# Packing six of eight head groups' outputs densely for the last query block's output projection

## The chip, the cores and the metric

The kernel runs on one core of one Trainium2 chip. The metric is the device time of one execution in microseconds; lower is better. Where several runs are given, the median is meant. TensorE is called PE, VectorE DVE, ScalarE ACT, GpSimd POOL and SyncE SP, as the profile does.

## What is computed

One transformer layer over 2048 tokens of width 640: layer norm, attention with 32 heads of 20 columns each, an output projection with `wo`, a residual sum; then a second layer norm, a bilinear GLU with hidden width 1728, its down projection and a second residual sum. Everything is bfloat16 from outside. The reference, cut:

```python
def _A_ref(x, wqkv, wo):
    qkv = (x @ wqkv).reshape(B, S, 3, H, Dh).transpose(2, 0, 3, 1, 4)
    q, k, v = qkv[0], qkv[1], qkv[2]
    p = softmax(einsum("bhqd,bhkd->bhqk", q, k) * (Dh ** -0.5))
    o = einsum("bhqk,bhkd->bhqd", p, v)
    return o.transpose(0, 2, 1, 3).reshape(B, S, D) @ wo
def _B_ref(x, w_gate, w_up, w_down):
    return ((x @ w_gate) * (x @ w_up)) @ w_down
h = x + _A_ref(layernorm(x), wqkv, wo)
out = h + _B_ref(layernorm(h), w_gate, w_up, w_down)
```

## The kernel before, in words

**Tiling.** The 2048 queries are four blocks of 512. The 32 heads are eight groups of four. A head has 20 rows, but it sits in a slot of 32 of the 128 partitions (`SLOT`), so that four heads fill one tile and PE can take a head's 32 rows alone; 12 rows of each slot are padding. Scores are computed transposed (128 keys by queries): L557 writes three banks of 512 columns of a score tile, ACT turns them into exponentials (L573), and L795 multiplies them with the values into the accumulator `acc`. Where the planner finds DVE free, one of the three banks is exponentiated by DVE instead with four operations (L610, L620, L621, L615), and ACT's instruction has 1024 columns instead of 1536.

**Passes.** The last block is block 3. Its group 0 is computed for all 512 queries (pass "3"), and groups 1 to 7 first for the first half of 256 queries (pass "A"), then for the second half (pass "B").

**Normalising.** The row sums of the softmax come out of the same matmul as the values. For most groups `norm` (L659) sends them out to DRAM (`sums`, L666) and back in another shape (`sums_all`, L667), takes reciprocals on DVE (L677), sends these out (`scr`, L679) and back to 32 partitions each (`bc`, four DMAs, L682), and then multiplies (L685) into `On[g]`, a 128 x 512 tile for each group, still in slots of 32 rows. The product is put in line seven score tiles later; the queue of DVE side work decides when it is done. Groups 7 of pass "A" and 6 and 7 of pass "B" are normalised without DRAM, by matmuls with an identity (L700, L716, L731, and L1391 in the tail).

**Projection.** `wo[g]` holds the output weights with the same padding: zeros, and 20 rows for each head (L987, L991). `out_mm` (L1047) adds eight matmuls for a tile of 128 queries and half of the 640 columns (L1052), and DVE adds the residual. For the first half of block 3 this is done by `job_quick`, which then takes the layer norm at once, while attention of pass "B" goes on. The second half is left to the tail.

**Tail.** `last_tail` (L1366) runs when all exponentials are done. For each of two tiles of queries and two halves of columns, `out_most` adds the residual by an identity matmul (L1376) and seven groups (L1378); `out_last` adds group 7 (L1382), which is normalised meanwhile: PE collects the sums (L700), DVE takes reciprocals and spreads them (L708, L710), PE turns them (L716), DVE multiplies (L1391). Then follow statistics (L209), the layer norm, the transposes, the GLU (L1203) and the down projection (L1270). Behind the projection stand 14 matmuls of a down projection held back for this, and warming matmuls (L1414), beside the layer norm.

**What sets the order.** The order on all engines is written by a planner in the kernel while the program is built: it keeps a model of the time at which PE, DVE and ACT get free, and puts jobs (projections, GLU, down projections) on PE between score tiles where its model leaves room. `later(n, fn)` lets something happen n score tiles later. Where PE's dense work gets thin in the model, it adds matmuls that keep PE's clock up (L508 and L553). All DMAs but the instruction loads go through SP's one queue, in program order; SP waits for what a DMA needs, and everything behind it waits too.

**Weights of the tail.** `load_last` (L1356) loads the rows of x for the last two tiles of queries and the GLU weights of parts 0 and 1 (four DMAs of 320 KB). The tail's GLU reads the resident parts 3 to 6 first, then 0, 1 and 2.

Of the kernel before, what the change touches and what calls it, by code (L numbers as in the profile page):

```python
# [10 lines left out]
BF16 = mybir.dt.bfloat16  # L11
# [5 lines left out]
ALU = mybir.AluOpType  # L17
AX = mybir.AxisListType

P = 128  # L20
# [3 lines left out]
DH = 20  # L24
NT = S // P
KT = D // P
FF = 1728
SLOT = 32
HPG = 4
NG = H // HPG  # L30
# [8 lines left out]
HALF = D // 2  # L39
FP = 7  # L40
FPW = 256
G1 = 4
SPLIT_G = {"1": 4, "2": 2, "3": 1}
QA = 3 * QB
RES0 = 3
# [29 lines left out]
ALONE_NS = {"out": 4350, "glu": 15260, "y": 5710}  # L75
PART_NS, TILE_NS, ROOM = 31500, 700, 2500
E_BUFS, E_LATE = 6, 2
SHIFT = 544.0
LOG2E = 1.4426950408889634
X_UNIT = 128.0  # L80
# [11 lines left out]
def kernel(  # L92
# [11 lines left out]
    nc = tc.nc  # L104
# [32 lines left out]
    wo = [const.tile([P, D], BF16, name=f"wo{g}") for g in range(NG)]  # L137
# [8 lines left out]
    On = [onp.tile([P, QB], BF16, name=f"on{g}") for g in range(NG)]  # L146
# [201 lines left out]
    for s, (p, g, lo, hi, _) in enumerate(segs):  # L348
        w = PASS[p][2]
        n = BANK // w  # L350
# [46 lines left out]
    def later(n, fn):  # L397
        events.append((now["i"] + n, fn))
# [257 lines left out]
    def read_out(b):  # L656
        return all(("om", b, t) in done for t in TAILS[b])

    def norm(s, asb):  # L659
        p, g = segs[s][0:2]  # L660
        b, c0, w = PASS[p]
        n = w // 32
        r16 = sums_all[:, col["n"]:col["n"] + n]
        col["n"] += n
        sums = dram.tile([HPG, w], F32, name="sums", tag=f"sums{w}")
        nc.sync.dma_start(sums[:], asb[DH:P:SLOT, 0:w])  # L666
        nc.sync.dma_start(r16, sums[:].rearrange("j (c f) -> (j c) f", f=n))  # L667

        due = at["dve"] + SUMS_NS

        def back():
            if at["pe"] < due and now["i"] < n_tiles:
                later(1, back)
                return
            ri = nrm.tile([P, n], F32, name="ri", tag=f"ri{n}")
            dve(130)
            nc.vector.reciprocal(ri[:], r16)  # L677
            scr = dram.tile([HPG, w], F32, name="scr", tag=f"scr{w}")
            nc.sync.dma_start(scr[:].rearrange("j (c f) -> (j c) f", f=n), ri[:])  # L679
            bc = nrm.tile([P, QB], F32, name="bc")  # L680
            for j in range(HPG):
                nc.sync.dma_start(bc[SLOT * j:SLOT * (j + 1), 0:w], scr[j:j + 1, :].to_broadcast([SLOT, w]))  # L682

            def times(asb, bc, p, g, c0, w):
                nc.vector.tensor_tensor(On[g][:, c0:c0 + w], asb[:, 0:w], bc[:, 0:w], ALU.mult)  # L685
                done.add(("n", p, g))
                yield 605 * w // QB

            def mult():
                if b and not read_out(b - 1):  # L690
                    later(1, mult)
                    return
                aux.append(times(asb, bc, p, g, c0, w))
            later(7, mult)
        later(4, back)
# [173 lines left out]
    m32, r = rstd_act(pair_mv[0], 2, lambda: bn(pair_mv[1], 0, xs[0][:, 2, :]))  # L869
# [11 lines left out]
    m32, r = rstd_act(pair_mv[1], 2)  # L881
# [103 lines left out]
    def load_wo():  # L985
        for g in range(NG):
# [6 lines left out]
            while at["pe"] < due and not now["forced"]:  # L993
                yield WAIT

    def make_identf():
        nc.vector.tensor_copy(identf[:], ident[:])

# [14 lines left out]
    late = {"res": {}, "next": {}}  # L1013
# [15 lines left out]
            nc.gpsimd.memset(late["Wd"][f][0:p0, :], 0.0)  # L1029
        nc.sync.dma_start(late["Wd"][f][p0:P, :], B_w_down[f * P:f * P + P - p0, :])  # L1030

    def new_st(rows_of):
        st = {"rows": rows_of, "xr": {}, "ln2T": late["ln2T"]}
        return st

    def load_tail(st, ts):
# [10 lines left out]
    def out_mm(on, st, t):  # L1047
        for hf in range(2):
            ps = bank()
            cs = slice(hf * HALF, (hf + 1) * HALF)  # L1050
            for g in range(NG):
                nc.tensor.matmul(ps[:, 0:HALF], lhsT=on[g][:, t * P:(t + 1) * P], rhs=wo[g][:, cs],  # L1052
                                 start=(g == 0), stop=(g == NG - 1))
                if g == NG - 1:
                    dve(408, 136)
                    nc.vector.tensor_tensor(st["h"][t][:, cs], ps[:, 0:HALF], st["xr"][t][:, cs], ALU.add)  # L1056
                yield 136
            done.add(("oh", t, hf))
            yield NEXT
# [76 lines left out]
    def job_out(on, st, ts, key):  # L1136
        pairs = [ts[k:k + 2] for k in range(0, len(ts), 2)]

        def T_pair(pair):
            for t in pair:  # L1140
                while end["pool"] is None and key is not None and (
                        ("l2", key, t) not in done or key in COLUMNS_OF and ("glu",) + COLUMNS_OF[key] not in done):
                    yield WAIT
                ensure_aux(("l2", key, t))
                if key is None:
                    yield from job_T(st["l", t], st["ln2T"][:, :, t * P:(t + 1) * P])
                    yield NEXT
                else:
                    nc.sync.dma_start(st["ln2T"][:, :, t * P:(t + 1) * P], st["l", t][:], transpose=True)
                    l2_at[key, t] = max(at["pe"], l2_at[key, t]) + TURN_NS  # L1150
            for t in pair:
                while end["pool"] is None and key is not None and at["pe"] < l2_at[key, t]:
                    yield WAIT
                ln2["rows"] -= 1
        done.difference_update({("l2", key, t) for t in ts})
        for k, pair in enumerate(pairs):
            for t in pair:
                yield from out_mm(on, st, t)
            if key is not None and k == len(pairs) - 1:
                done.add(("om",) + key)  # L1160
            aux.append(ln2_pieces(st, pair, key))
            if k:
                yield from T_pair(pairs[k - 1])
        yield from T_pair(pairs[-1])

    def w_tile(src, fp, wt):
        w = min(FPW, FF - fp * FPW)
        view = wt[:, 0:KT * FPW].rearrange("p (c f) -> p c f", f=FPW)
        nc.sync.dma_start(view[:, :, 0:w], src[:, fp * FPW:fp * FPW + w].rearrange("(c p) f -> p c f", p=P))
# [124 lines left out]

    def rows(b, ts):
        if b not in tail_st:
            tail_st[b] = new_st(rows_of(b))
            tail_st[b]["res"] = late["res"]
        load_tail(tail_st[b], ts)
        rows_in.add((b, ts[0]))  # L1300
# [55 lines left out]
    def load_last():  # L1356
        st = tail_st[LAST_B]
        load_tail(st, LAST_T)
        load_w(0, st)
        load_w(1, st)  # L1360

    def run(gen):
        for _ in gen:
# [2 lines left out]
    def last_tail():  # L1366
# [6 lines left out]
        def out_most(t, hf):  # L1373
            ps = ps_h[t, hf] = bank()
            cs = slice(hf * HALF, (hf + 1) * HALF)
            nc.tensor.matmul(ps[:, 0:HALF], lhsT=ident[:], rhs=st["xr"][t][:, cs], start=True, stop=False)  # L1376
            for g in range(NG - 1):
                nc.tensor.matmul(ps[:, 0:HALF], lhsT=on[g][:, t * P:(t + 1) * P], rhs=wo[g][:, cs], start=False, stop=False)  # L1378

        def out_last(t):  # L1380
            for hf in range(2):
# [131 lines left out]


    def general():
        st = new_st(None)
        st["res"] = {}
        with tc.For_i(0, S, P) as r0:
            st["rows"] = lambda t: bass.ds(r0, P)
# [2 lines left out]
            for g in range(NG):  # L1522
# [42 lines left out]
                nc.vector.tensor_copy(On[g][:, 0:P], ps[:])  # L1565
# [36 lines left out]
```

## Time and profile before

| | |
|---|---|
| median of 3 runs | 896.7 us (895.01 to 898.06) |
| the profiled execution | 900.67 us |
| its span, first to last instruction | 898.8 us |
| mean granted clock of PE | 0.989 |
| end of the last exponential | about 858.8 us |
| tail behind it | about 35 us |

The profile is one execution. Busy time is counted per engine; a line such as L573 is a line of the kernel; "idle before" is idle time of the engine just ahead of an instruction and what ended it. The granted clock is the share of full speed that PE was given. Matmul ends are modelled, so a group of pipelined matmuls is best read by the distance between starts. In a row with "x7" the length covers all seven. The planner's stretch of pass "A" and "B" and the tail are the parts that matter here.

### The profile page before, as it was taken

The page shows a single profiled execution, that of the slowest core. Times are in us where ns is not written, and L with a number is a line of the kernel's source. Part 1 is how long each engine was busy: PE and PEld are TensorE (multiplying, and loading weights), DVE is VectorE, ACT ScalarE, POOL GpSimd, SP SyncE. Part 2 cuts the span into 40 slices and gives each one's busy share as a digit, 9 for nine tenths or more (in the row PEclk, how much of TensorE's full clock was granted, in tenths as well). Part 3 has the DMA queues.
Part 4 walks back from the last instruction along what each step waited for, and adds up shares of the span by engine and source line. Part 5 has one row for each costly group of instructions (what it writes and reads, how often), then busy time and mean ns, then how long its engine had stood idle before and what let it go on. Part 6 is the DMA issues. An engine that isn't in the chain of part 4 may idle for free.

```text
span 898.8 us, 21965 instructions
## 1 busy us (share of the span) xinstructions
PE 813.7 (91%) x8921; PEld 374.1 (42%) x8921; DVE 773.7 (86%) x1448; ACT 852.7 (95%) x719; POOL 31.4 (3%) x122
## 2 busy tenths in 40 slices
PE   7889999989999899889999998998899999999997
PEld 5333232222233344544444554443434455444465
DVE  7778899999999899789999998999889988889842
ACT  6999999999999999989999999999999999999951
POOL 4100000000002000001000000001000000000000
PEclk9999999999999999989999999999989999999999
DMA  6030010011034556432214334111441312010310
GB/s 198 25 65 2 1 28 25 15 36 28 14 84 112 122 146 198 112 88 66 54 51 122 81 96 107 47 30 29 121 121 45 85 31 74 15 44 9 94 38 18
DMA packets 110763, 60.15 MB, mean 67 GB/s; under 512 B 37976, under 2 KB 107652, under 8 KB 110656
## 3 DMA queue, kind: packets, MB, share of 16 engines
q1 hardware_dynamic: 110656, 58.68, 25.0%
q8 instruction: 72, 1.18, 0.6%
q14 instruction: 35, 0.29, 0.1%
HBM read 48.09 MB, written 7.28 MB: 62 GB/s over the span
## 4 chain that ended last, share of the span: by engine, by line
ACT 56%; PE 21%; issue 13%; DVE 9%; DMA 1%; SPq 0%; ACTq 0%; DVEq 0%
ACT E L573 46%; ACT El L573 10%; PE sc L557 5%; PE mi L1221 3%; PE acc L795 3%; PE f L1203 2%; PE mi L306 1%; PE mi L1052 1%; DVE xv L610 1%; PE mi L1270 1%; PE f L1270 1%; DVE xt L620 1%; DVE xt L621 1%; DVE xe L615 1%; DVE hh L1229 1%
## 5 line engine op out<-in xcount | busy, mean ns | idle before, releaser
L573 ACT ACTIVATE E<-sc 128x1536 bf16<-128x1536 f32 (+1 forms) x560 | 694.0, 1387 | 7.3 <-PE sc L557 6.0
L557 PE MATMUL sc<-qa,kT 32*128 32x256 bf16 (+1 forms) x2176 | 204.1, 320 | 23.8 <-ACT E L573 13.5
L557 PEld LDWEIGHTS <-kT 32*128 32x128 bf16 x3136 | 85.2, 92 | 223.9 <-issue 193.4
L610 DVE TENSOR_SCALAR xv<-sc 128x512 f32<-128x512 f32 x199 | 137.1, 690 | 47.3 <-PE sc L557 44.4
L573 ACT ACTIVATE El<-sc 128x1536 bf16<-128x1536 f32 (+1 forms) x123 | 159.7, 1371 | 0.6 <-PE sc L557 0.5
L795 PE MATMUL acc<-E,vx 128*32 128x256 bf16 (+1 forms) x2245 | 158.2, 315 | 0.6 <-DVE vx L271 0.6
L615 DVE SCALAR_TENSOR_TENSOR xe<-xt,xv 128x512 int16<-128x512 f32 x199 | 134.3, 681 | 0.8
L621 DVE SCALAR_TENSOR_TENSOR xt<-xt,xv 128x512 f32<-128x512 f32 x199 | 133.2, 680 | 0.6
L620 DVE SCALAR_TENSOR_TENSOR xt<-xv 128x512 f32<-128x512 uint16 x199 | 132.1, 679 | 0.3 <-DVE ri L677 0.2
L306 PE MATMUL mi<-lnT,wp 128*128 128x512 bf16 x305 | 86.5, 381 | 7.1 <-DVE qa L313 3.4
L795 PEld LDWEIGHTS <-vx 128*32 128x32 bf16 x3136 | 62.2, 96 | 62.5 <-issue 60.6
L557 PE MATMUL sc<-qb,kT 32*128 32x256 bf16 (+1 forms) x960 | 69.0, 283 | 3.4 <-ACT E L573 2.2
L1270 PE MATMUL mi<-wd,hh 128*128 128x320 bf16 x378 | 65.5, 301 | 1.1 <-DVE xr L1274 1.0
L1221 PE MATMUL mi<-ln2T,wg 128*128 128x256 bf16 x390 | 56.7, 274 | 8.6 <-DVE u L1226 7.2
L1221 PE MATMUL mi<-ln2T,wu 128*128 128x256 bf16 x390 | 55.5, 274 | 7.4 <-DVE hh L1229 7.2
L795 PE MATMUL acc<-El,vx 128*32 128x256 bf16 (+1 forms) x579 | 60.6, 294 | 0.5 <-ACT El L573 0.5
L795 PE MATMUL acc<-xe,vx 128*32 128x256 bf16 (+1 forms) x312 | 57.3, 306 | 0.0
L1270 PEld LDWEIGHTS <-hh 128*128 128x128 bf16 x448 | 37.9, 97 | 29.5 <-issue 18.2
L1221 PEld LDWEIGHTS <-wg 128*128 128x128 bf16 x390 | 33.6, 97 | 30.0 <-issue 25.3
L306 PEld LDWEIGHTS <-wp 128*128 128x128 bf16 x310 | 24.8, 97 | 50.6 <-issue 38.5
L1221 PEld LDWEIGHTS <-wu 128*128 128x128 bf16 x390 | 33.8, 97 | 28.3 <-issue 25.1
L1052 PE MATMUL mi<-wo,on 128*128 128x320 bf16 x224 | 41.6, 312 | 2.3 <-DVE xr L1056 2.2
(152 smaller groups left out, 623.0 us busy)
## 6 DMA issues: line engine op xcount, KB each, us to landing
wu<-in_B_w_up_dram SPq DMA_DIRECT2D x38, 320.0 KB
wg<-in_B_w_gate_dram SPq DMA_DIRECT2D x37, 320.0 KB
bc<-scr SPq DMA_DIRECT2D x60, 64.0 KB
bc<-scr SPq DMA_DIRECT2D x108, 32.0 KB
qsp<-qa SPq DMA_DIRECT2D x8, 384.0 KB
xr<-in_A_x_dram SPq DMA_DIRECT2D x16, 160.0 KB
out_dram<-xr SPq DMA_DIRECT2D x14, 160.0 KB
wd<-in_B_w_down_dram SPq DMA_DIRECT2D x13, 160.0 KB
```

The costliest lines, as they stand in the source:

```text
L306: nc.tensor.matmul(ps[:], lhsT=wslice(m, g, c), rhs=lnT[:, c, ch * QB:(ch + 1) * QB], start=(c == 0), stop=(c == KT - 1))
L557: nc.tensor.matmul(sc[:, o:o + w], lhsT=kT[g][SLOT * j:SLOT * (j + 1), kt * P:(kt + 1) * P], rhs=q_of(g, b, c0, w)[SLOT * j:SLOT * (j + 1) ...
L573: exps = nc.scalar.activation(e[:, 0:n_act], sc[:, 0:n_act], ACT.Exp, bias=EXP_BIAS, scale=SM_SCALE)
L610: took = nc.vector.tensor_scalar(v[:], ps, X_SCALE, X_BASE, ALU.mult, ALU.max)
L615: nc.vector.scalar_tensor_tensor(e[:], t[:], X_R, v[:], ALU.mult, ALU.add)
L620: lambda: nc.vector.scalar_tensor_tensor(t[:], u, X_P, u, ALU.add, ALU.mult),
L621: lambda: nc.vector.scalar_tensor_tensor(t[:], t[:], X_Q, u, ALU.add, ALU.mult),
L795: nc.tensor.matmul(acc["t"][SLOT * j:SLOT * (j + 1), 0:w], lhsT=vx[kt][:, VS * h:VS * h + SLOT], rhs=e, start=(acc["n"][j] == 0), stop=(ac ...
L1052: nc.tensor.matmul(ps[:, 0:HALF], lhsT=on[g][:, t * P:(t + 1) * P], rhs=wo[g][:, cs], start=(g == 0), stop=(g == NG - 1))
L1203: nc.tensor.matmul(ps[:, 0:n], lhsT=st["w", fp][k][:, c, f_cols(fp, f2)], rhs=st["ln2T"][:, c, c0:c0 + n], start=(c == 0), stop=(c == KT - 1))
L1221: nc.tensor.matmul(ps[:, f2 * n:(f2 + 1) * n], lhsT=st["w", fp][k][:, c, f_cols(fp, f2)], rhs=st["ln2T"][:, c, c0:c0 + n], start=(c == 0), ...
L1270: nc.tensor.matmul(ps[:, 0:HALF], lhsT=st["hh"][f // 2][:, f % 2, t * P % HW:t * P % HW + P], rhs=late["Wd"][f][:, cs], start=(f == 0), st ...
```

## The change

Only the last block, and there only groups 0 to 5 (24 heads, 480 rows). The product L685 of such a group no longer goes to `On[g]` but to `On[4]` or `On[5]`, by turns. From there `pack` sends each head's 20 rows by DMA to their dense place: row 20 h of a stack of `On[0]` to `On[3]`. Where a head crosses a multiple of 128 it takes two DMAs. `On[0]` to `On[3]` then hold 128, 128, 128 and 96 rows without padding. The padded weights `wo[0]` to `wo[3]` are overwritten with 480 dense rows, three to six score tiles after the last projection of block 2. The projections of block 3 then add six terms (four dense ones, and groups 6 and 7 as before) instead of eight, the tail's `out_most` five instead of seven. Groups 6 and 7 are not packed. The fallback `general` is changed in the same way; it does not run on these inputs.

The four weight loads of `load_last` are no longer issued together, but 0, 3, 6 and 9 score tiles later.

```diff
+N_PACK = 6
+PACKED_ROWS = (128, 128, 128, 96)
+WO_AT, LAST_STEPS = 3, 3
...
+    def pack(o, g, cols):
+        for j in range(HPG):
+            r, d = DH * (HPG * g + j), 0
+            while d < DH:
+                to = (r + d) % P
+                n = min(DH - d, P - to)
+                nc.sync.dma_start(On[(r + d) // P][to:to + n, cols], o[SLOT * j + d:SLOT * j + d + n, cols])
+                d += n
...
             def times(asb, bc, p, g, c0, w):
-                nc.vector.tensor_tensor(On[g][:, c0:c0 + w], asb[:, 0:w], bc[:, 0:w], ALU.mult)
+                packed = b == LAST_B and g < N_PACK
+                o = On[4 + g % 2 if packed else g]
+                nc.vector.tensor_tensor(o[:, c0:c0 + w], asb[:, 0:w], bc[:, 0:w], ALU.mult)
+                if packed:
+                    pack(o, g, slice(c0, c0 + w))
...
+    def load_packed(k):
+        nc.sync.dma_start(wo[k][0:PACKED_ROWS[k], :], A_wo[P * k:P * k + PACKED_ROWS[k], :])
+
+    def out_terms(packed):
+        return [(k, n) for k, n in enumerate(PACKED_ROWS)] + [(g, P) for g in range(N_PACK, NG)] if packed else [(g, P) for g in range(NG)]
...
-            for g in range(NG):
-                nc.tensor.matmul(ps[:, 0:HALF], lhsT=on[g][:, t * P:(t + 1) * P], rhs=wo[g][:, cs],
+            for g, n in out_terms(st["packed"]):
+                nc.tensor.matmul(ps[:, 0:HALF], lhsT=on[g][0:n, t * P:(t + 1) * P], rhs=wo[g][0:n, cs],
...
                 done.add(("om",) + key)
+                if key == (LAST_B - 1, 2):
+                    for n in range(len(PACKED_ROWS)):
+                        later(WO_AT + n, lambda n=n: load_packed(n))
...
-        load_w(0, st)
-        load_w(1, st)
+        for fp in range(2):
+            two = st["w", fp] = []
+            for m, src in enumerate((B_w_up, B_w_gate)):
+                later(LAST_STEPS * (2 * fp + m), lambda fp=fp, src=src, nm=("wu", "wg")[m], two=two: two.append(
+                    w_tile(src, fp, late["w"].tile([P, KT * FPW], BF16, name=nm))))
...
-            for g in range(NG - 1):
-                nc.tensor.matmul(ps[:, 0:HALF], lhsT=on[g][:, t * P:(t + 1) * P], rhs=wo[g][:, cs], start=False, stop=False)
+            for g, n in out_terms(True)[:-1]:
+                nc.tensor.matmul(ps[:, 0:HALF], lhsT=on[g][0:n, t * P:(t + 1) * P], rhs=wo[g][0:n, cs], start=False, stop=False)
```

More of the change, by code (lines that the diff above doesn't have):

```diff
@@ L1030, in load_wd, with new_st @@
         nc.sync.dma_start(late["Wd"][f][p0:P, :], B_w_down[f * P:f * P + P - p0, :])
-    def new_st(rows_of):
-        st = {"rows": rows_of, "xr": {}, "ln2T": late["ln2T"]}
+    def new_st(rows_of, packed):
+        st = {"rows": rows_of, "xr": {}, "ln2T": late["ln2T"], "packed": packed}
         return st
@@ L1296, in rows @@
         if b not in tail_st:
-            tail_st[b] = new_st(rows_of(b))
+            tail_st[b] = new_st(rows_of(b), b == LAST_B)
             tail_st[b]["res"] = late["res"]
@@ L1515, in general @@
     def general():
-        st = new_st(None)
+        st = new_st(None, True)
         st["res"] = {}
@@ L1564, in general @@
                 nc.tensor.transpose(ps[:], oq[:].rearrange("p j e -> p (j e)"), ident[:])
-                nc.vector.tensor_copy(On[g][:, 0:P], ps[:])
+                o_t = On[4 + g % 2 if g < N_PACK else g]
+                nc.vector.tensor_copy(o_t[:, 0:P], ps[:])
+                if g < N_PACK:
+                    pack(o_t, g, slice(0, P))
             for fn in (job_out(On, st, [0], None), job_glu(st, [0]), job_y(st, [0])):
```

## The prediction

> **What bounds the kernel now.** I read the page first: its first line, the busy shares, and the group of the projection's matmuls.
>
> ```profile
> span 898.8 us, 21965 instructions
> PE 813.7 (91%) x8921; PEld 374.1 (42%) x8921; DVE 773.7 (86%) x1448; ACT 852.7 (95%) x719; POOL 31.4 (3%) x122
> L1052 PE MATMUL mi<-wo,on 128*128 128x320 bf16 x224 | 41.6, 312 | 2.3 <-DVE xr L1056 2.2
> ```
>
> ACT, which makes the exponentials, is busy 95%, PE 91%: an average that says nothing about the stage that is changed. The change takes 8 of the 224 projection matmuls of L1052 away, and 8 of the tail's. So the second view is the busy time by stretch (engines in the order PE, PEld, DVE, ACT, POOL with instruction counts, then granted clock, DMA share, GB/s), from the first projection of the last block to the end of the tail's projection.
>
> ```profile
> 771.00:790.00 19.00, 17.82 (x239) 8.22 (x238) 17.66 (x45) 19.00 (x17) 1.25 (x2) 1.00 0.01 2
> 790.00:810.00 20.00, 18.09 (x264) 9.60 (x261) 16.67 (x31) 20.00 (x17) 0.00 (x0) 1.00 0.21 49
> 810.00:830.00 20.00, 17.80 (x265) 9.77 (x259) 18.63 (x33) 20.00 (x18) 0.00 (x0) 1.00 0.05 10
> 830.00:850.00 20.00, 18.39 (x259) 9.13 (x256) 17.46 (x32) 19.77 (x17) 0.00 (x0) 1.00 0.40 106
> 859.00:865.00 6.00, 6.00 (x52) 4.52 (x47) 2.68 (x10) 1.26 (x2) 0.00 (x0) 1.00 0.01 3
> ```
>
> From 771 to 850 ACT has 0.23 us of 79 free: there only less work for ACT moves the end. From 859 on PE is busy without a gap, 6.00 of 6.00. The chain that ended last, in order of time (start, length, what), confirms both.
>
> ```profile
> 857.62 1.15 ACT El L573
> 859.45 0.95 PE f L1378 x7
> 860.40 0.34 PE f L700 x4
> 860.89 0.95 PE f L1378 x7
> 861.84 0.44 PE acc L716 x4
> 862.42 0.95 PE f L1378 x7
> 863.78 0.95 PE f L1378 x7
> ```
>
> The last exponential hands over to PE, and all four groups of seven L1378 matmuls stand in the chain.
>
> **The change part by part.** The built program's order of instructions on each engine is unchanged up to the first projection of the last block, except that DMAs are put into SP's queue. From there on the planner lays the work out anew.
>
> *Eight matmuls less in the tail.* Each L1378 group takes 0.95 us for seven, 0.136 us each; five are left, so each of four groups gives 0.27 us if nothing else ends late. What is late next is read from VectorE's timeline.
>
> ```profile
> 859.24 0.42 DVE L807 COPY asb<-acc 128x256 f32<-128x256 f32 x1 [5.98 <-PE acc L795]
> 860.83 0.21 DVE L708 RECIPROCAL ri<-f 128x8 f32<-128x8 f32 x1 [1.17 <-PE f L700]
> 861.07 0.29 DVE L710 COPY bc<-ri 128x256 f32<-128x256 f32 x1
> 861.55 0.55 PEld L716 LDWEIGHTS acc<-identf,bc 128*128 128x128 f32 x4
> 862.33 0.48 DVE L1391 TENSOR_TENSOR on<-asb,acc 128x128 bf16<-128x128 f32 x2 [0.89 <-PE acc L716]
> 863.55 0.90 DVE L209 BATCH_NORM_STATS2 st<-f 128x6 f32<-128x320 f32 x2 [0.74 <-PE f L1382]
> 864.91 0.89 DVE L209 BATCH_NORM_STATS2 st<-f 128x6 f32<-128x320 f32 x2 [0.22 <-PE f L1382]
> 851.60 0.29 DVE L710 COPY bc<-ri 128x256 f32<-128x256 f32 x1
> 852.09 0.52 PEld L716 LDWEIGHTS mi<-identf,bc 128*128 128x128 f32 x4 [0.48 <-PE sc L557]
> ```
>
> Group one ends 0.27 earlier; the copy L807 ends at 859.66, so L700 (860.40 less 0.27) is not held. Then L710 ends at 861.36 - 0.27 = 861.09, and the last two rows show that L716 starts loading 0.20 after an L710 (852.09 against 851.89): 861.29, which is 0.26 before its 861.55. So group two gives nothing: its two matmuls were the cover of the reciprocal. Group three gives 0.27 (the product L1391 moves with L716), group four 0.27: 0.80. Last, the second statistics L209, at 864.91, would start at 864.11, but the first pair, moved by 0.53, ends with its aggregate near 864.16. That leaves **0.75 us**, and everything behind (layer norm, transposes, GLU) shifts by it. If all covers held it would be 8 x 0.136 = 1.09; if groups three and four too ended on VectorE, 0.27.
>
> *Eight matmuls less in the attention stretch.* Eight such matmuls stand in the first row below in 1.26 us; without them PE gets about that, while ACT is full: nothing by itself. But the planner fills in differently. In the changed program VectorE takes 200 of the 512-column banks of scores instead of 199, ACT has 482 tiles of 1536 columns and 201 of 1024 instead of 483 and 200: one bank less on ACT.
>
> ```profile
> 772.98 1.26 PE L1052 MATMUL mi<-wo,on 128*128 128x320 bf16 x8
> L573 ACT ACTIVATE E<-sc 128x1536 bf16<-128x1536 f32 x39 | 54.9, 1478 | 0.0
> L573 ACT ACTIVATE E<-sc 128x1024 bf16<-128x1024 f32 x15 | 15.4, 1038 | 0.2 <-ACT E L573 0.2
> ```
>
> By mean length that is 1478 - 1038 = 440 ns, by busy share 54.9/39 - 15.4/15 = 0.38 us. I take **0.44**, the upper, because ACT is saturated there; bounds 0 (a new wait eats it) and 0.44. The four VectorE operations that the bank costs lie in its free time: in that stretch it is busy 70.4 of 79 us.
>
> *Outputs by staging tile and 50 pack DMAs* (27 pieces, of which 23 go twice, once for each half of the block). VectorE's product is the same instruction, written elsewhere. SP's issue cost and the small transfers' latency are bounded by these rows:
>
> ```profile
> 845.96 1.72 SPq L682 DMA_DIRECT2D bc<-scr  x4
> SPq L682 <- DMA scr<-ri: 17.9, 11, 3.4
> 693.13 1.60 DMA sums<-asb
> 838.28 0.50 SPq L666 DMA_DIRECT2D sums<-asb  x1
> 841.20 0.34 SPq L667 DMA_DIRECT2D sums_all<-sums  x1
> ```
>
> 0.43 us an issue: 21.5 us of SP in all, four or five issues (1.7 to 2.2 us) a group. Such a transfer is not in the trace; it lands in 1.60 us like the small `sums`, or at worst 3.4 like the longest wait for `scr`; I take 1.6. The new wait is that a group's first pack waits in SP's queue for the product; behind it stand sums, rows and weights of later groups, whose products come some seven tiles on, so at most 2.2 us goes into that distance. Who could wait is PE: the first projection reads the first half's packs. The last packed product of that half was at 758.15 (row below); its end, four issues and 3.4 us make 763.7, and the projection starts at 772.98: 9 us of cover. In the second half the last two packed products stand, in the changed order, a few operations ahead of group 6's copy (851.60), at about 848. Nine issues (3.9), a weight load's 0.5 between them and 3.4 give 855.8; PE reads from 859.0 (859.45 less 0.44): 3 us of cover. Cost 0; without the cover each late microsecond is one of the end.
>
> ```profile
> 758.15 0.41 DVE L685 TENSOR_TENSOR on<-asb,bc 128x256 bf16<-128x256 f32 x1
> 656.95 1.28 SPq L1169 DMA_DIRECT2D qa<-in_B_w_gate_dram  x1
> 680.33 0.51 SPq L666 DMA_DIRECT2D sums<-asb  x1
> L1052 PEldq EVENT_SEMAPHORE  x9: 51/51/51, 262.9 to 264.2; - x9
> 263.29 1.12 PE L1052 MATMUL mi<-wo,on 128*128 128x320 bf16 x7
> ```
>
> *Output weights anew.* Four loads stand in SP's queue between the last resident weight (issued by 658.2) and the sums at 680.33, where SP is empty; their first reader is at 772.98. Cost 0.
>
> *Waits on PE.* The tail's first group must now wait for many DMA semaphores, seven extra instructions of 51 ns. The first projection of block 0 carried nine of them, and its seven matmuls still took 1.12 us, no more than eight in 1.26 without. Bounds 0 and 7 x 0.051 = 0.36; I take 0.
>
> *Weights spaced.* Before, the four loads stood together ahead of the sums of 838.28, whose second hop was issued 2.92 us later (841.20), though the first takes 1.60 by the row of 693.13. Up to 1.3 us is given back, but VectorE, whose reciprocal reads the sums, is no bound there, and ACT was full: 0. The last of the four is issued nine tiles later, near 847, and read after 880.
>
> **Sum:** 0.75 + 0.44 = 1.2 us. The profiled execution took 900.67 (898.8 and 1.87 around it), so 899.5; the runs' median is 896.7, so **895.5**. About 0.3% (2.7 us) is what a measurement of this kernel can tell from no change; 1.2 is 0.13%.
>
> **The rivals.**
>
> ```profile
> 400.00:410.00 10.00, 9.88 (x114) 4.32 (x112) 8.04 (x15) 7.70 (x8) 0.00 (x0) 0.79 0.01 2
> 650.00:660.00 10.00, 9.01 (x52) 3.38 (x53) 7.67 (x16) 8.56 (x8) 0.00 (x0) 0.67 1.14 304
> 654.00:656.00 2.00, 2.00 (x11) 1.14 (x13) 1.40 (x3) 1.65 (x2) 0.00 (x0) 0.50 1.14 292
> ```
>
> A, *it does less than it says*: the attention end stands, and the tail's matmuls only uncover VectorE: 0.27 us, 896.4. For it: group two already gives nothing. Against it: PE's full 6.00 of 6.00.
>
> B, *a half-clock stretch in the new order of the attention*. At 400 and 650 the granted clock falls (0.50 within 654 to 656), PE can't feed ACT, and ACT loses 2.30 and 1.44 us. The projections are dense 128-row work; with fewer of them, the new order may meet such a stretch between 771 and 859, where there is none now. 1.4 to 2.3 against the gain of 1.2: 896.9 to 897.8. Against it: the planner puts in as many warming matmuls: 112 on the projection's bank become 116, 18 on the scores' banks become 14.
>
> C, *slower: the half clock falls into the tail*, 859 to 893, where PE is the bound. A mean of 0.67 over ten is 6.6 us at half speed; PE then loses 3.3: 898.8, and with B's 2.3 as well 901.1. It decides from 2.4 us at half clock on, where the loss passes the 1.2. For it: eight dense matmuls are gone there, and a wait of 0.2 us ahead of L716 is new. Against it: the tail ran at 1.00, and the fillers of the layer norm stay. [...]
>
> D, *faster by more*: the stretches of 400 and 650 may differ between executions (the three runs span 3 us), and the changed kernel meets one less: 1.4 to 2.3 beside the 1.2: 893.2 to 894.1. Against it: everything ahead of 771 keeps its order on PE.
>
> **How the numbers follow.** Forecast 0.46, A 0.18, B 0.12, C 0.12, D 0.12. Faster than 894.0: most of D and the forecast's own scatter (the three runs span 3 us), 0.20. Slower than 899.4: the larger half of C, some of B, 0.13. Within: 0.67. The range goes from D's low end, 893.2, to C's first price with some of the runs' scatter, which is where slower begins: 899.4.
>
> **What would show it.** Right: five L1378 matmuls of 0.68 us a group, L716 0.19 to 0.2 after L710 with PE idle before it; from the end of the last exponential to the end of the chain 0.75 us less; ACT busy all of 771 to 858; 201 short exponentials; no wait of PE for a pack. Wrong: PE waiting for a DMA at the first L1378 or L1052, idle ACT between 771 and 858, or a clock under 1.00 behind 771.

## The result and the profile after

| | before | after |
|---|---|---|
| median of 6 runs each | 896.15 us (895.01 to 898.38) | 905.55 us (902.43 to 909.21) |
| ratio to before, 95% interval | 1 | 1.0104 (1.0082 to 1.0127) |
| the profiled execution | 900.67 us | 902.43 us |
| its span | 898.8 us | 900.6 us |

The change costs 9.4 us at the medians. The forecast was 895.5 us. The profiled execution of after is the fastest of its six, that of before is slower than all of its six, so the two traces are compared stretch by stretch and not by their ends.

First the head of the page of after, and the group of the projection:

```profile
span 900.6 us, 21981 instructions
PE 802.5 (89%) x8848; PEld 373.5 (41%) x8905; DVE 776.3 (86%) x1452; ACT 852.0 (95%) x719; POOL 31.4 (3%) x122
L1074 PE MATMUL mi<-wo,on 128*128 128x320 bf16 x216 | 38.4, 303 | 2.6 <-DVE xr L1078 2.5
```

The eight matmuls are gone (216, was 224), and the page says nothing more. The busy time by stretch does (columns as in the prediction: PE, PEld, DVE, ACT, POOL, granted clock, DMA share, GB/s):

```profile
710.00:720.00 10.00, 7.66 (x115) 4.02 (x116) 7.06 (x12) 8.25 (x7) 0.00 (x0) 0.97 0.34 90
720.00:730.00 10.00, 9.32 (x99) 4.49 (x94) 5.01 (x10) 7.64 (x7) 0.00 (x0) 0.69 0.07 16
771.00:790.00 19.00, 14.62 (x186) 6.47 (x191) 16.84 (x43) 17.01 (x14) 1.11 (x2) 0.92 0.00 1
790.00:810.00 20.00, 17.92 (x260) 9.35 (x259) 15.23 (x28) 18.76 (x15) 0.00 (x0) 0.91 0.14 35
810.00:830.00 20.00, 18.31 (x264) 10.31 (x263) 18.07 (x32) 20.00 (x18) 0.00 (x0) 1.00 0.11 27
830.00:850.00 20.00, 18.65 (x262) 9.69 (x262) 18.04 (x33) 20.00 (x18) 0.00 (x0) 1.00 0.26 69
```

ACT, full from 771 to 850 before, now loses 1.99 us from 771 to 790 and 1.24 from 790 to 810; before that it loses 1.75 and 2.36 from 710 to 730, a stretch that the forecast did not look at. The granted clock falls to 0.69 and 0.91.

For a comparison that does not depend on what happened earlier in an execution, I cut both traces at the same two instructions: from the 571st instruction of ACT, an exponential ahead of the first packed product, to the end of the last exponential. Each stretch holds the same number of ACT instructions (x126). Before, then after:

```profile
704.85:858.76 153.91, 141.34 (x1984) 73.54 (x1984) 128.59 (x245) 153.68 (x126) 1.25 (x2) 1.00 0.18 45
```

```profile
698.55:861.00 162.45, 143.76 (x1967) 74.51 (x1976) 131.06 (x249) 154.19 (x126) 1.11 (x2) 0.96 0.18 46
```

The stretch takes 162.45 us instead of 153.91, 8.54 more, and ACT idles 8.26 us of it (162.45 less 154.19) instead of 0.23. So the loss lies here. That the instruction starts at 704.85 in one execution and at 698.55 in the other is not the change: up to there the order of instructions on PE, DVE and ACT is the same in both.

**The first wait.** SP's queue of after around the first packed products (start, length, instruction):

```profile
699.26 2.56 SPq L1171 DMA_TRANSPOSE ln2T<-ln  x2
701.91 6.84 SPq L668 DMA_DIRECT2D on<-on  x9
708.86 0.42 SPq L1305 DMA_DIRECT2D out_dram<-xr  x1
709.38 0.37 SPq L691 DMA_DIRECT2D scr<-ri  x1
710.91 1.72 SPq L694 DMA_DIRECT2D bc<-scr  x4
712.72 0.40 SPq L1194 DMA_DIRECT2D wu<-in_B_w_up_dram  x1
```

Nine packs stand in a row and hold SP for 6.84 us. The products of groups 0 and 1 both wait until block 2's projection has read `On`, and then come directly behind one another. From the transposes to the issue of the GLU weights `wu` it is 13.46 us (712.72 less 699.26). Before, in the same place:

```profile
705.75 2.56 SPq L1149 DMA_TRANSPOSE ln2T<-ln  x2
...
716.56 0.40 SPq L1169 DMA_DIRECT2D wu<-in_B_w_up_dram  x1
```

10.81 us, so `wu` is now issued 2.65 us later; 4.2 of the 6.84 go into time in which SP waited anyway. Who reads `wu`, from PE's timeline of before and then of after (in brackets the idle time ahead of the instruction, and its end):

```profile
722.12 0.71 PE L1221 MATMUL mi<-ln2T,wu 128*128 128x256 bf16 x5 [0.51 <-DVE hh L1229]
```

```profile
717.65 0.72 PE L1246 MATMUL mi<-ln2T,wu 128*128 128x256 bf16 x5 [2.35 <-DMA wu<-in_B_w_up_dram]
```

After, PE stands still for 2.35 us until the load lands, 4.88 us behind its issue (a piece of the chain of after, from 712.72). With the same 4.88 the load of before would land at 721.44, 0.68 ahead of its reader at 722.12. Its landing is not in the trace; with the 4.22 and 4.59 us of the late loads of e2 and e9 below, the cover would be 1.34 and 0.97. So it was about 1 us, against a delay of 2.65. Behind the gap in PE the granted clock falls to one half (after, the stretch ahead of the fall and the fall itself):

```profile
715.92:719.33 3.41, 1.68 (x26) 1.01 (x30) 2.25 (x4) 1.66 (x2) 0.00 (x0) 1.00 0.17 40
719.33:726.16 6.83, 6.60 (x66) 2.92 (x54) 1.82 (x4) 5.16 (x4) 0.00 (x0) 0.50 0.03 6
```

The clock falls near 719 in the three profiled executions in which `wu` comes late (after, e2, e9), and in none of the other eleven. At half speed PE can't feed ACT: ACT loses 1.75 us up to 720, by the wait, and 2.36 from 720 to 730, most of it by the clock.

The cost of a pack's issue, first all fifty, then two single ones, of 20 and of 16 rows:

```profile
L668 SPq DMA_DIRECT2D on<-on x50: 554/707/1456, 701.9 to 857.5; - x50
```

```profile
742.45 0.71 SPq L668 DMA_DIRECT2D on<-on  x1
749.42 0.55 SPq L668 DMA_DIRECT2D on<-on  x1
```

The median is 0.707 us and not the 0.43 that I took from `bc`; 3.0 to 3.8 us a group, 36 us in all, or some 38 with the short breaks between issues.

**The second wait.** SP of after, the same place before, then DVE of after:

```profile
746.42 3.56 SPq L668 DMA_DIRECT2D on<-on  x5
750.08 0.52 SPq L1194 DMA_DIRECT2D wu<-in_B_w_up_dram  x1
750.70 0.47 SPq L1194 DMA_DIRECT2D wg<-in_B_w_gate_dram  x1
751.26 0.47 SPq L691 DMA_DIRECT2D scr<-ri  x1
754.71 1.73 SPq L694 DMA_DIRECT2D bc<-scr  x4
```

```profile
751.05 0.34 SPq L679 DMA_DIRECT2D scr<-ri  x1
753.45 1.73 SPq L682 DMA_DIRECT2D bc<-scr  x4
```

```profile
758.09 0.43 DVE L699 TENSOR_TENSOR on<-asb,bc 128x256 bf16<-128x256 f32 x1 [1.69 <-DMA bc<-scr]
```

The packs push two weight loads of 320 KB directly ahead of `scr`; from the issue of `scr` to that of `bc` it is then 3.45 us, where before it was 2.40, `bc` comes late, and DVE, which before had no idle time at this product, waits 1.69 us with everything behind it. ACT loses 1.77 us from 730 to 780. Loads directly ahead of `scr` make it late without any packs, too: at 696.70 of before, where two loads were issued 1.1 and 1.5 us ahead of it, `bc` follows 3.78 us later.

**The tail** went as forecast. From the chain of after:

```profile
859.91 1.10 ACT El L576
861.70 0.68 PE f L1406 x5
862.88 0.68 PE f L1406 x5
864.32 0.68 PE f L1406 x5
865.41 0.68 PE f L1406 x5
894.44 0.49 DVE xr L1299
```

and the last row of before's:

```profile
893.09 0.49 DVE xr L1274
```

Four groups of five, 0.68 us each. The distances of their starts are 0.26, 0.09 and 0.27 us shorter than before and the last group is 0.27 shorter, where the forecast had 0.27, nothing, 0.27 and 0.27. From the end of the last exponential to the end of the last DVE operation it is 33.93 us (861.00 to 894.93), before 34.82 (858.76 to 893.58): 0.89 less. No matmul waits for a pack.

### The profile page after: what moved, and what is told of

Same layout as the page of the kernel before. It is cut to its first block, busy times and chain, and to the rows that moved or that the text cites. A ratio compares the mean times of both kernels' runs of the same rounds, so it can differ in the third digit from the quotient of the medians.

```text
span 900.6 us, 21981 instructions
## 1 busy us (share of the span) xinstructions
PE 802.5 (89%) x8848; PEld 373.5 (41%) x8905; DVE 776.3 (86%) x1452; ACT 852.0 (95%) x719; POOL 31.4 (3%) x122
## 4 chain that ended last, share of the span: by engine, by line
ACT 54%; PE 20%; issue 14%; DVE 10%; DMA 2%; SPq 0%; ACTq 0%; DVEq 0%
ACT E L576 44%; ACT El L576 9%; PE sc L560 5%; PE mi L1246 3%; PE acc L811 3%; PE mi L1295 2%; PE f L1228 2%; DVE xv L613 2%; PE mi L309 1%; PE f L1295 1%; DVE xt L624 1%; DVE xe L618 1%; DVE xt L623 1%; DVE u L1251 1%; PE mi L324 1%
## 5 line engine op out<-in xcount | busy, mean ns | idle before, releaser
L309 PE MATMUL mi<-lnT,wp 128*128 128x512 bf16 x280 | 82.7, 381 | 8.1 <-DVE qa L316 3.4
L1074 PE MATMUL mi<-wo,on 128*128 128x320 bf16 x216 | 38.4, 303 | 2.6 <-DVE xr L1078 2.5
```

Source lines behind the costliest of these rows:

```text
L309: nc.tensor.matmul(ps[:], lhsT=wslice(m, g, c), rhs=lnT[:, c, ch * QB:(ch + 1) * QB], start=(c == 0), stop=(c == KT - 1))
L1074: nc.tensor.matmul(ps[:, 0:HALF], lhsT=on[g][0:n, t * P:(t + 1) * P], rhs=wo[g][0:n, cs], start=(g == 0), stop=(g == NG - 1))
```

## The experiments

Theory Q: the packs hold SP's queue, and what stands behind them comes late. Rival O: fewer matmuls in the first projection make the planner lay out another order, which idles PE and ACT whatever the packs do. Further candidates were the transfers themselves, the reloaded weights and the spaced loads. For each run the table gives the median with its ratio to the runs of before on the same chip, and from the profiled execution the stretch between the two ACT instructions named above, ACT's idle time in it, and the time from the last exponential to the last DVE operation. The last three columns are of one execution each.

| run | edit | median us | ratio (95%) | stretch us | ACT idle us | tail us |
|---|---|---|---|---|---|---|
| before | | 895.4 to 896.6 | 1 | 153.91 | 0.23 | 34.82 |
| after | | 905.55 | 1.0104 (1.0082 to 1.0127) | 162.45 | 8.26 | 33.93 |
| e1 | after, no packs | 897.80 | 1.0014 (0.9990 to 1.0037) | 155.81 | 2.54 | 33.93 |
| e2 | before, packs into a spare tile | 901.38 | 1.0068 (1.0041 to 1.0095) | 160.15 | 5.59 | 34.82 |
| e3 | after, 11 whole packs | 898.28 | 1.0023 (1.0001 to 1.0046) | 155.64 | 2.48 | 34.28 |
| e4 | after, packs on GpSimd | 899.45 | 1.0034 (1.0009 to 1.0060) | 156.10 | 2.70 | 34.20 |
| e5 | second half packed, SP | 898.42 | 1.0032 (1.0014 to 1.0051) | 154.36 | 0.49 | 34.00 |
| e6 | second half packed, GpSimd | 895.95 | 1.0010 (0.9994 to 1.0026) | 153.92 | 0.23 | 34.42 |
| e7 | after, packs spread | 904.55 | 1.0086 (1.0058 to 1.0113) | 158.80 | 4.95 | 33.96 |
| e8 | e4 with eight terms | 896.78 | 1.0015 (0.9998 to 1.0032) | 154.57 | 0.69 | 34.35 |
| e9 | after, first nine on SP only | 902.74 | 1.0064 (1.0033 to 1.0094) | 161.80 | 7.71 | 34.21 |
| e10 | after, first nine on GpSimd | 905.70 | 1.0131 (1.0071 to 1.0190) | 159.08 | 4.94 | 33.93 |
| e11 | before, loads spaced | 898.61 | 1.0028 (1.0008 to 1.0048) | 153.94 | 0.23 | 34.82 |
| e12 | before, six terms | 899.25 | 1.0029 (1.0009 to 1.0049) | 155.78 | 2.60 | 34.82 |

**e1, no packs.**

```diff
                 nc.vector.tensor_tensor(o[:, c0:c0 + w], asb[:, 0:w], bc[:, 0:w], ALU.mult)
-                if packed:
-                    pack(o, g, slice(c0, c0 + w))
```

> The changed kernel without its 50 pack DMAs: the six products still go to the two staging tiles, but nothing is copied from there, so the projections of the last block read stale rows; every instruction of PE, VectorE, ACT and GpSimd stays in the order of the changed kernel. Theory Q (SP's queue is held by the packs, 37 us in all and 6.84 us at 702, and weights, rows and x behind them come late): the loss of 9.4 us goes, 894 to 897. Rival O (the planner's new order, with eight matmuls fewer at 773, leaves PE idle and drops its clock, whatever the packs do): 903 to 907, and ACT still loses its 1.14 us in 780 to 790. If both share it: 898 to 902.

897.80, between Q's range and the shared one: 7.75 us of the 9.4 go with the packs. That is Q. But the time does not fall below before, and the stretch shows why (e1):

```profile
703.15:858.96 155.81, 139.73 (x1967) 73.61 (x1976) 131.07 (x249) 153.27 (x126) 1.11 (x2) 0.99 0.17 45
```

ACT still idles 2.54 us, all of it between 780 and 800. Both theories hold a part.

**e2, the packs alone.** The order of before, the fifty copies into a tile that nobody reads.

```diff
                 nc.vector.tensor_tensor(On[g][:, c0:c0 + w], asb[:, 0:w], bc[:, 0:w], ALU.mult)
+                if b == LAST_B and g < N_PACK:
+                    pack(On[g], g, slice(c0, c0 + w))   # into the spare tile
```

> The kernel before, with the same 50 pieces copied behind the same products into a spare tile that nobody reads; projections, output weights, the tail and the weight loads as before. Q: slower by most of the loss, 901 to 907, with a wait for the GLU weights near 713 to 720. O: 895 to 898, as before.

901.38, in Q's range. The stretch of e2, and PE's wait for the weights:

```profile
698.65:858.80 160.15, 144.17 (x1977) 74.36 (x1984) 128.73 (x245) 154.56 (x126) 1.25 (x2) 0.97 0.18 47
717.34 0.72 PE L1234 MATMUL mi<-ln2T,wu 128*128 128x256 bf16 x5 [1.94 <-DMA wu<-in_B_w_up_dram]
```

6.24 us longer than before's, without any other part of the change. ACT idles 5.36 us more, 3.70 at the first wait and 1.67 at the second. Its busy time is 0.88 longer: instructions that follow one another without a gap overlap by about 0.1 us (1.45 long, starts 1.35 apart), and each of the eight gaps takes such an overlap away. Nothing is lost from 780 to 800.

**e3, eleven packs instead of fifty.** Same queue, same waits for the products.

```diff
     def pack(o, g, cols):
-        for j in range(HPG):
...
+        nc.sync.dma_start(On[g % 4][:, cols], o[:, cols])
```

> The changed kernel with one DMA of 128 partitions for each product in place of four or five of up to 20 (11 instead of 50; the rows land undensely, so the last block's projection adds up the wrong rows). Q, if the number of issues counts: SP's hold falls from 37 us to some 8, the two first products take 1.5 instead of 6.84 us, and the time is 894 to 898. If what counts is a wait of the queue for the product or the landing of the DMA and not the issues: 902 to 907. O: 903 to 907.

898.28, 0.28 over the range of the first reading and as without packs. The wait of the queue for a product, and the bytes (more than in after: all 128 rows), cost next to nothing; what costs is the time that the issues take. Its issues:

```profile
L663 SPq DMA_DIRECT2D on<-on x11: 477/494/1050, 702.3 to 846.4; - x11
```

A DMA of 128 rows takes SP 0.49 us, one of 20 rows 0.71. The tail is 0.35 us longer than in after by an operation of the GLU; its projection is as in after.

**e4, the same fifty on GpSimd.**

```diff
-                nc.sync.dma_start(On[(r + d) // P][to:to + n, cols], ...)
+                nc.gpsimd.dma_start(On[(r + d) // P][to:to + n, cols], ...)
```

> The changed kernel with its 50 pack DMAs issued by GpSimd, which is idle there (POOL is busy 3%), instead of SP: same bytes, same pieces, SP's queue as without packs. Q: 894 to 897. If the transfers themselves disturb (DMA engines, ports) or land later than 3 us behind their product: 899 to 907, with PE waiting for them at the first projection matmul of the tail. O: 903 to 907.

```profile
L668 POOL DMA_DIRECT2D on<-on x50: 502/507/760, 699.4 to 848.6; - x50
```

899.45, and a stretch of 156.10, 0.29 from that of e1: 50 transfers beside the others cost ACT next to nothing. The median, over Q's range, is 1.65 us above e1's, and the intervals of the two overlap; the trace shows 0.27 us of it in the tail, where ten semaphore instructions of 51 ns stand at the first group on PE (after has seven, e1 none, and the same tail). PE waits for no pack there, which was the sign of the other reading. Whether the rest of the 1.65 us is a cost of the packs is open. For these transfers of 2 to 20 KB an issue takes SP 0.71 us (median, after); from issue to landing those of e4 between 840 and 860 take 1.7 (seven of 10 KB) to 2.6 us. The time of fifty issues is what costs.

**e5 and e6, only the second half packed.** Group 0's product is written in two halves, of which the second is packed; the first projection keeps its eight padded terms, and the dense weights are loaded behind it. 27 packs.

```diff
+                for h0 in (range(0, QB, HW) if b == LAST_B and w == QB else (c0,)):
+                    packed = b == LAST_B and g < N_PACK and h0 == HW
...
-            tail_st[b] = new_st(rows_of(b), b == LAST_B)
+            tail_st[b] = new_st(rows_of(b), False)
```

> Only the second half of the last block is packed (27 pack DMAs on SP instead of 50: group 0's product is written in two halves, of which the second is packed); the first half keeps the padded rows and its eight matmuls per projection, the output weights are loaded dense after that projection, and ACT's exponentials stand in the order of the kernel before. From the runs so far the loss is some 7.8 us of packs on SP and some 2.5 us of ACT idle in 780 to 800 by the planner's new order, against 0.9 us gained in the tail. If both are right (Q and O): the 2.5 us at 780 to 800 are gone, and SP is held at 702 by four issues of 2.9 us instead of nine of 6.84, so the GLU weights come in time: 895 to 897. If any pack on SP costs in proportion to its issues: 27 of 50, 899 to 901.

> As the run before it in the list (only the second half packed), with the 27 pack DMAs issued by GpSimd. Q and O: 895 to 896, 0.9 us under the kernel before by the tail alone. If packs issued by GpSimd cost something themselves (the whole change with packs on GpSimd had 899.45 against 897.8 without packs): 896.5 to 898.

e6 has 895.95, in the range of "Q and O", and a stretch equal to before's; the tail is 0.40 us shorter and not 0.9, with twelve semaphore instructions at its first group. That can't be told from before (0.9994 to 1.0026). e5 has a stretch of 154.36, so four packs in place of the nine leave the weights in time, but its median is 898.42, above the expected 895 to 897. Its ten runs fall into two groups, 895.7 to 897.3 at granted clocks of 0.995 to 0.997, and 899.6 to 902.5 at 0.987 to 0.992. The profiled one, the slowest, has all its 20.5 us at half speed ahead of 700, and so starts the stretch late, at 705.50; its stretch is at full clock. So its packs account for at most 0.45 us of this execution; the other slow ones have no trace.

**e7, the packs spread.** Each pack in a `later` of its own; the nine come 8 to 17 tiles later.

```diff
-                nc.sync.dma_start(...)
+                one = lambda ...: nc.sync.dma_start(...)
+                later(apart + k // (1 if now["i"] + 12 < n_tiles else 2), one)
```

> The changed kernel with all 50 packs on SP, but one at a tile of the planner instead of four, five or nine in a row: the nine of groups 0 and 1 come 8 to 17 tiles later, behind the GLU weights or between them, those of groups 2 and 3 six tiles later, the others from the next tile on (two a tile near the end). SP's issue time stays some 35 us. If what counts is what stands behind a row of packs (weights, scr): 897 to 899.5, near the 897.8 without packs. If the total hold of SP counts wherever the packs stand: 902 to 906.

904.55, median of four: the reading that only what stands behind a row of packs counts falls. ACT is full from 710 to 730, so the first wait is gone. The second stays in another form, by the edit itself: near 758 a product (L705 in e7) waits 1.9 us until the late packs have left its staging tile. And a new place appears in e7, directly ahead of the tail:

```profile
855.00:860.00 5.00, 4.24 (x44) 1.89 (x45) 2.20 (x6) 4.66 (x4) 0.00 (x0) 0.73 0.05 10
```

The granted clock falls there to 0.73, as it does in the next pair in one of two.

**e9 and e10, the two waits apart.** Nine packs on SP and 41 on GpSimd, then the other way round.

```diff
+        q = nc.sync if cols.start == 0 and g < 2 else nc.gpsimd
-                nc.sync.dma_start(...)
+                q.dma_start(...)
```

> The changed kernel with only the nine packs of the first two products on SP, the other 41 on GpSimd. If the two waits of the changed kernel are separate, this run has the first alone: GLU weights late near 713 to 718, granted clock under 1.00 near 720, ACT idle 4.1 us there (1.75 and 2.36 in the changed kernel) beside some 2.4 us in 780 to 800, and no wait for the norm rows near 755: 902 to 904, against 899.45 with all packs on GpSimd. If the first wait costs nothing by itself: 899 to 900.

> The other half: the nine packs of the first two products on GpSimd, the other 41 on SP. Separate waits: ACT full in 710 to 730, scr and bc late near 751 to 758, ACT idle some 1 to 1.8 us in 760 to 780 beside the 2.4 of 780 to 800: 900 to 902. If the late norm rows are only an after-effect of the first wait: 899 to 900, with no wait near 755.

e9 has 902.74, as expected: `wu` is waited for 2.5 us, the clock is 0.66 from 720 to 730, ACT idles 4.25 us at this first wait (4.11 in after), and there is no wait near 755. Its stretch of 161.80 is 5.70 longer than e4's, but not all of that is the first wait: from 780 to 800 ACT idles 3.26 us and not 2.40; the half clock lasts 6.83 us there and not 3.41. e10's trace has the late norm rows (1.1 us of ACT from 730 to 780), so this wait is no after-effect of the first. Its stretch of 159.08 is 2.98 longer than e4's, 1.04 of it again from 780 to 800. So the two halves add up to more than the 6.35 us by which after's stretch exceeds e4's, and the shares of the waits are to be read at their places. The median of e10, 905.70 of four runs, is far over the expected 900 to 902. The trace shows one place more, again ahead of the tail (e10):

```profile
853.00:858.00 5.00, 5.00 (x51) 1.86 (x52) 1.23 (x3) 4.63 (x4) 0.00 (x0) 0.66 0.29 74
```

PE is busy 5.00 of 5.00 us at a clock of 0.66, and ACT loses 0.37 us. The rest of e10's median is open.

**e8 and e12, the order.** e8 gives the first projection of e4 two more terms, e12 takes two terms from before's.

```diff
-            for g, n in out_terms(st["packed"]):
+            for g, n in first_terms(st["packed"]):   # e8: 6 + 2 terms
```

```diff
-            for g in range(NG):
+            for g in ((0, 1, 2, 3, 6, 7) if st is tail_st.get(LAST_B) else range(NG)):   # e12
```

> The changed kernel with its packs issued by GpSimd, and the first projection of the last block back at eight matmuls a bank: two that multiply the staging tiles with the old output weights of groups 4 and 5 are added (so the first half of the last block is wrong by these terms); tail with six as in the changed kernel. O (fewer matmuls there make the planner's order in which VectorE takes six banks in a row and ACT waits for the row sums' matmuls in 780 to 800): ACT has no idle time in 780 to 800, and the time falls by 2 to 2.5 us against 899.45: 896.5 to 897.5. If the 780 to 800 loss has another cause: 899 to 900.

> The kernel before with one edit: the first projection of the last block leaves out the terms of groups 4 and 5 (its first half is wrong by them), six matmuls a bank instead of eight. No staging, no packs, no new weights; VectorE and ACT then have the order of the changed kernel, instruction for instruction. O: ACT loses some 2.4 us in 780 to 800 with VectorE over 9 of 10 busy there, and the run is 1.5 to 2.5 us over the kernel before: 897 to 899. If the loss in 780 to 800 needs the packs, the staging or the reloaded weights: ACT full there, 895 to 896.5.

O holds, from both sides: with eight terms ACT is full from 780 to 800, and the stretch is 154.57 (e4: 156.10); with six, and nothing else of the change, it is 155.78, as in e1:

```profile
700.60:856.38 155.78, 139.70 (x1967) 73.61 (x1976) 131.08 (x249) 153.18 (x126) 1.11 (x2) 0.99 0.17 45
```

The median of e12, 899.25, is 0.25 over its expected range. The reloaded weights and the staging tiles therefore cost nothing that the trace can show (155.81 against 155.78). My picture of the mechanism in these expectations, six banks in a row for VectorE, was wrong. The timeline of e12 shows another:

```profile
784.79 0.41 DVE L807 COPY asb<-acc 128x256 f32<-128x256 f32 x1
785.26 0.62 PE L795 MATMUL acc<-El,vx 128*32 128x256 bf16 x8 [1.29 <-DVE asb L807]
785.94 2.48 ACT L573 ACTIVATE El<-sc 128x1024 bf16<-128x1024 f32 x2 [1.83 <-PE acc L795]
```

There is one accumulator. Its copy L807 stands in DVE's queue behind exponential work, PE waits 1.29 us for it with no other matmul to do, and ACT waits 1.83 us for PE to free an `El` tile. Another 0.77 us are lost behind it, where the clock is at one half (785.13 to 788.54). Before, the copy at 787.18 held nobody. Why the planner's layout brings the end of a segment and DVE's exponentials together with six terms and not with eight was not tried.

**e11, the spaced loads alone.**

```diff
-        load_w(0, st)
-        load_w(1, st)
+                later(LAST_STEPS * (2 * fp + m), lambda ...: two.append(w_tile(src, fp, ...)))
```

> The kernel before with nothing but the four first weight loads of the tail spaced by three tiles. Costed at nothing in the forecast: 895 to 898, ACT idle at most 0.4 us in 700 to 858. If the spacing takes part in the loss: over 899.

The stretch is 153.94 and ACT idles 0.23, both as before: the spacing does nothing behind 700, and ahead of 700 it changes nothing. The median is still 898.61, over the expected 898, with an interval that excludes 1. Its executions have a median granted clock of 0.992, those of before on the same chip 0.997, and in the profiled one all 13.7 us at half speed lie ahead of 700. So intervals of this kind leave out some of the scatter between executions, and a ratio of 1.003 here is no evidence without a trace that shows the place.

## Why the prediction was wrong

**What held.** The tail: five matmuls in 0.68 us, 0.89 gained where 0.75 was forecast, no wait for a pack. The bank moved from ACT to DVE: ACT's busy time in the stretch is 153.18 in e12 and 153.68 before, 0.50 less where 0.44 was forecast. (In after it is 0.51 more, because each gap takes an overlap away.) Output weights anew, 0: e1 against e12, 0.03 us. Weights spaced, 0: e11, 0.03 us. Waits on PE, 0: seven semaphore instructions in after, and its first group still starts 0.7 us behind the last exponential (861.00 to 861.70; before 858.77 to 859.45). The bound of 51 ns each would have been no bound for more of them: with ten (e4, e8, e9) the tail takes 0.27 to 0.42 us more than in after, with twelve (e6) 0.49.

**Outputs by staging tile and 50 pack DMAs, costed 0.** This step failed, and it is the main one: 6.24 us of the stretch by e2, 7.75 us of the median by e1. Three of its figures were off. An issue takes 0.71 us and not 0.43: I priced DMAs of 20 rows by one of 32 rows, the nearest in form, though only 1.6 times too low. "Four or five issues a group" became nine in a row, because two products wait for the same event; the row of packs is then 6.84 us and not 2.2. The decisive one is "behind it stand sums, rows and weights of later groups, whose products come some seven tiles on": I measured the cover by the reader of the rows and none by the reader of the weights, PE's GLU, which had about 1 us (0.68 to 1.34, by the load time taken). The rows of before held the answer: the issue of `wu` at 716.56, a first use at 722.12, and a load time.

**Eight matmuls less in the attention stretch, +0.44.** The bank was there and the new order ate it: 2.37 us more idle time of ACT, net 1.87 us (e12). The rival B foresaw the sort of loss (a stretch at a lower clock in the new order, 1.4 to 2.3 us), and gave it 0.12. With Q taken away the time is B's: 897.8 measured in e1, 896.9 to 897.8 forecast. That is in part luck: B put the loss on the clock, and in e12 1.83 of the 2.60 us are a wait for the accumulator's copy, which the half clock follows. What I read as safety, that ACT was full and the planner fills in, is no measure of it: a full ACT has no reserve against a PE that runs out of work for 1.3 us.

**The sum by the runs.** Packs 6.24 (e2) and order 1.87 (e12) make 8.11; the stretch of after is 8.54 longer. Less 0.89 in the tail that is 7.65. The medians differ by 9.4, with an interval of 7.3 to 11.4. Whether the difference between 7.65 and 9.4 is a further drop of the clock ahead of the tail, as in e7 and e10, in the slower executions of after, is not shown. They do have a lower granted clock (0.980 at 909.21 us, 0.990 at 902.43), but only the fastest is traced, and it has no drop there.

**The clock.** The first gap in PE cost ACT nearly twice its length: 2.35 us of waiting made 1.75 us of ACT's loss, the lower clock behind it most of 2.36 us more. A mean of 0.83 over 10 us, as from 770 to 780 and from 790 to 800 of after, is 3.4 us at half speed. PE was not idle all the time ahead of the fall near 719: it waited 2.35 us, and was busy 1.68 of the last 3.41 us. Sparse work was enough. How sparse can't be read from these traces: half speed followed 3.41 us with 2.52 busy (before, up to 397.44), and did not follow 3.41 us with 2.07 busy (after, up to 784.18). No run leaves out the matmuls that the planner adds for the clock, so what they do for it is not shown. One kernel loses a different amount in each execution (after: granted clocks of 0.980 to 0.990 in six); why is open.

## What to carry to other kernels

Before you put DMAs into a queue that works in order, list what stands behind them, and take for each the time from its issue to its first reader less its landing: the smallest of these is the cover (about 1 us here), to be set against the longest row of issues at the price of DMAs with the same number of rows. Here the trace shows next to no cost for the same small copies when an idle engine issues them (0.29 us of the stretch, e4 against e1). Taking matmuls from an engine that feeds a full one can cost more than they took when a planner's order changes with them (1.87 us net for 1.26 us of matmuls, e12), so look in the new order for who runs out of work, not for who got less to do.

## What the runs showed of the hardware

SP's issue of an SBUF to SBUF copy does not follow its rows: 0.49 us for 128 rows (e3), and in after 0.63 for 4, 0.67 for 8, 0.71 for 12, 0.55 to 0.60 for 16 and 0.71 for 20. GpSimd issued the same pieces in 0.51 us each (e4). The pieces of 16 rows and the whole 128 are the shortest here, but no run varied the rows alone, and why the others take longer is open.

In 14 profiled executions the 571st instruction of ACT started between 698.25 and 705.50 us, with the same instructions ahead of it on PE, DVE and ACT, and from the last DVE operation to the end of the span, in which the last store lands, it took 4.7 us (e2) to 7.7 (e10). Both scatter by more than the 0.89 us that the tail gained, so such a gain can be read in a trace and not in a time.

In these traces PE's clock is either full or half, and each stretch at half speed ahead of the end of the work is 3.41 or 6.83 us long. In the profiled execution of before all 17.1 us of it lie ahead of 700, in the part that the change leaves alone; in that of after all 13.7 us lie behind. Over the 92 executions of before that were timed beside the experiments, the time goes with the mean granted clock: 893.5 to 895.7 us at 0.998, 901.9 at 0.986, and a straight line through all rises by 0.6 us for each 0.001 (correlation -0.95).
